# Weights converted ahead of the first scores, and places of their own for the beginning and for each batch's preparation

## The chip, the core and the metric

The kernel runs on one core of a Trainium2 chip. A core has five engines with instruction queues of their own: TensorE (PE: matmuls; its weight loads are shown as PEld), VectorE (DVE), ScalarE (ACT), GpSimd (POOL) and SyncE (SP), which here only issues DMA transfers. SBUF is the working memory with 128 partitions; matmuls write to PSUM, of which a partition has eight banks of 2 KB. Each engine takes its instructions in the order in which they were recorded and waits on semaphores for what it needs. The metric is the time of one execution on the device in microseconds (us), the median of three runs.

## The reference

Two layers follow each other, for 4 batches of 12288 positions with 128 channels. The first is an attention over 768 pooled positions that serve as keys and values at once, the second a gated feed-forward layer with a token shift.

```python
kv_pool = kv.reshape(B, H // r, r, W // r, r, C).mean(axis=(2, 4))     # r = 4: means over 16
k = v = kv_pool.reshape(B, -1, C) @ w_sr                               # 768 x 128 a batch
s = (q @ k.transpose(0, 2, 1)) / sqrt(C)
a = exp(s - s.max(-1, keepdims=True)); a /= a.sum(-1, keepdims=True) + 1e-9
x = a @ v
x_prev = x shifted by one position (0 in front)
xk = mu_k * x + (1 - mu_k) * x_prev;  xr = mu_r * x + (1 - mu_r) * x_prev
k = maximum(xk @ w_k, 0);  v = (k * k) @ w_v                           # 128 -> 1024 -> 128
out = v / (1 + exp(-(xr @ w_r)))
```

The feed-forward weights come in double precision; all else is single precision.

## The kernel before, in words

Precision is kept by splitting: a factor is held as a high part in the format fp32r, which TensorE takes at full rate, and a low part that is the remainder (names end in h and l). A product is then three matmuls, low x high, high x low, high x high. The probabilities are split into two fp16 halves (pp), the values into v1 and v2.

A batch is cut into 24 tiles of 512 positions, 96 tiles in all. For one tile (plan_tile):

- qf is loaded and split into qh (ScalarE) and ql (GpSimd). For each of four groups of 128 positions, S0 to S3 (six matmuls: three over 512 keys, three over 256) give the scores in PSUM. VectorE takes the negated maximum nm, ScalarE the exponential pe with its sum, VectorE the reciprocal (dn, rc), ScalarE the first half of the probabilities (f1) and VectorE the second (f2: scalar_tensor_tensor into pp). A DMA transposes pp into pT (tt).
- AV0 to AV5 (18 matmuls px<-pT,v) form the attention's output. ScalarE scales it into xe, VectorE forms the differences d, xk and xr and the high part xkh, ScalarE xrh, GpSimd the low parts xkl and xrl.
- ha and hb (24 matmuls ph<-...) form the hidden layer in four pairs of 128 rows. ScalarE takes the Relu rr and its square kh in fp32r, VectorE the product of ph and rr (the square, kk), and kk - kh = kl comes from GpSimd (from VectorE in the fourth pair).
- z (three matmuls pz<-...) forms the gate, worked out by ScalarE and VectorE (g). va and vb (24 matmuls pv<-...) form the second product; VectorE multiplies it by g into o, which a DMA stores.

A tile is 93 matmuls. PSUM is used in three pools: ps_b has three buffers of two banks for all big results (S, ph, pk, pt), ps_x one bank (px and pz), ps_v one bank (pv). A new tile of ps_b takes the buffer of an earlier one and waits until its last reader is done.

The order is written out by hand: the table WHEN gives each step a time, step s of tile i is recorded at i x PERIOD + WHEN[s] (note, plan: a heap sorted by time), and every engine executes in the order of recording. At any time TensorE works on four tiles: scores of one, px of the one before, ph and pv of older ones. The numbers only order the steps; nothing waits for a time.

Beside the tiles stand three more things, written as generators that yield waiting times (steps, until):

- batch_prep(0), the beginning: first_keys loads the first batch's windows in 16 loads; VectorE adds the two windows of each (two), TensorE multiplies by w_sr into pk, split makes ks, ksh and ksl.
- weights / load_weights: a part of 512 columns of w_k, w_v (two parts each) or 128 of w_r comes as pairs of 32-bit words. VectorE forms exponent and mantissa (e, ef, ei, m, six instructions), ScalarE the low word as a number (lf) and the high part (hi), GpSimd three instructions: rest, dw = top - hi, lo = dw + rest. w_k is converted from WK_AT on, w_v and w_r after the first S.
- batch_prep(1) to (3): later_keys loads the next batch's windows in 12 parts, one in each of 12 tiles, and VectorE adds them (acc<-kv_t); then pk (TensorE), ks (ScalarE), ksh (VectorE), ksl (GpSimd), the scale (am, ex, exi, exs, ivs, sv: one column but for am), ksv, the transposes pt (TensorE), and v1 (ScalarE) and v2 (VectorE) out of them. pk and pt are both put at the phase PK_AT of a tile.

All recorded steps have one line, that of the helper Ordered (L33), so the rows below are told apart by names.

Of the kernel before, what the change touches and what calls it, by code (L numbers as in the profile page):

```python
# [20 lines left out]
class Ordered:  # L21


    on = True

# [3 lines left out]
    def __getattr__(self, name):  # L29
        op = getattr(self.engine, name)  # L30

        def call(*args, **kwargs):
            ins = op(*args, **kwargs)  # L33
            return self.tc.keep_in_program_order(ins) if Ordered.on else ins

        return call
# [3 lines left out]
def tile_kernel(ctx, tc, qT, kv0, kvw, w_sr, mu_k, mu_r, w_k, w_v, w_r, outT):  # L40
    nc = tc.nc
    P = 128
# [38 lines left out]
    def load_weights(raw, hi, lo, half, gap):  # L81

        n = raw.shape[1]
        l32, h32 = raw[:, :, 0], raw[:, :, 1]
        e = work.tile([P, n], I32, name="e", tag="rr", bufs=2)
        dve.tensor_scalar(e, h32, 20, 0x7FF, op0=ALU.logical_shift_right, op1=ALU.bitwise_and)
        lf = work.tile([P, n], F32, name="lf", tag="kl", bufs=3)
        act.activation(out=lf, in_=l32.bitcast(mybir.dt.uint32), func=AF.Copy, scale=2.0 ** -52)
        yield gap
        least = 897.0 if half else 896.0  # L90
        ef = work.tile([P, n], F32, name="ef", tag="kh", bufs=3)
        dve.tensor_scalar(ef, e, least, least + 255.0, op0=ALU.max, op1=ALU.min)
# [12 lines left out]
        yield gap
        top = m.bitcast(F32)
# [9 lines left out]
    def split(c0, c1, pk, ks, ksh, ksl):  # L116

        act.activation(out=ks[:, c0:c1], in_=pk[:, c0:c1], func=AF.Copy, scale=scale / WIN)
        dve.tensor_copy(out=ksh[:, c0:c1], in_=ks[:, c0:c1])
        dve.tensor_tensor(  # L120
            out=ksl[:, c0:c1], in0=ks[:, c0:c1], in1=ksh[:, c0:c1].bitcast(F32), op=ALU.subtract
        )

    def first_keys(ks, ksh, ksl):

        pk = ps_b.tile([P, 1024], F32, name="pk", tag="big")
        for c0, c1 in CHUNKS:
            for w in range(0, WIN, 2):
                kv_t = prep.tile([P, 2, c1 - c0], F32, name="kv_t", tag="kv", bufs=KV_BUFS)
                sp.dma_start(out=kv_t, in_=kv0[:, w:w + 2, c0:c1])  # L130
                two = work.tile([P, T], F32, name="two", tag="az", bufs=2)[:, 0:c1 - c0]
                dve.tensor_tensor(out=two, in0=kv_t[:, 0, :], in1=kv_t[:, 1, :], op=ALU.add)
                pe.matmul(pk[:, c0:c1], lhsT=wsr, rhs=two, start=(w == 0), stop=(w == WIN - 2))
                yield 1.0
            split(c0, c1, pk, ks, ksh, ksl)

    def later_keys(b, ks, ksh, ksl):

        acc = prep.tile([P, K], F32, name="acc", tag="acc")
        for c0 in range(0, K, KC):  # L140
            kv_t = prep.tile([P, KC, WIN], F32, name="kv_t", tag="kv", bufs=KV_BUFS)
            sp.dma_start(out=kv_t, in_=kvw[b - 1, :, c0:c0 + KC, :])
            yield until(BR_AT, 6.0)
            dve.tensor_reduce(out=acc[:, c0:c0 + KC], in_=kv_t, axis=AX.X, op=ALU.add)
        yield until(PK_AT, 4.0)
        pk = ps_b.tile([P, 1024], F32, name="pk", tag="big")
        for c0, c1 in CHUNKS:
            pe.matmul(pk[:, c0:c1], lhsT=wsr, rhs=acc[:, c0:c1], start=True, stop=True)
        yield 2.0
        act.activation(out=ks, in_=pk[:, 0:K], func=AF.Copy, scale=scale / WIN)  # L150
        yield 3.0
        dve.tensor_copy(out=ksh, in_=ks)
        yield 3.0
        pool.tensor_tensor(out=ksl, in0=ks, in1=ksh.bitcast(F32), op=ALU.subtract)

    def batch_prep(b, res):

        later = b > 0
        ks = prep.tile([P, K], F32, name="ks")
        ksh = bat.tile([P, K], F32R, name="ksh")  # L160
        ksl = bat.tile([P, K], F32R, name="ksl")
        yield from later_keys(b, ks, ksh, ksl) if later else first_keys(ks, ksh, ksl)
        res += [ksh, ksl]
        yield V_WAIT if later else 4.0
        am = prep.tile([P, 1], F32, name="am")
        dve.tensor_reduce(out=am, in_=ks, axis=AX.X, op=ALU.max, apply_absolute_value=True)
        yield 3.0
        ex = prep.tile([P, 1], F32, name="ex")
        dve.tensor_scalar_max(ex, am, 2.0 ** -90)
        yield 2.0  # L170
        exi = prep.tile([P, 1], I32, name="exi")
        dve.tensor_single_scalar(exi, ex.bitcast(I32), 0x7F800000, op=ALU.bitwise_and)
        yield 2.0
        exs = prep.tile([P, 1], F32, name="exs")
        dve.tensor_scalar_mul(exs, exi.bitcast(F32), 2.0 ** -14)
        yield 2.0
        ivs = prep.tile([P, 1], F32, name="ivs")
        dve.reciprocal(ivs, exs)
        sv = bat.tile([P, 1], F32, name="sv")
        dve.tensor_scalar(sv, exs, 2.0 ** -15, 1.0 / scale, op0=ALU.mult, op1=ALU.mult)  # L180
        yield 2.0
        ksv = prep.tile([P, K], F32, name="ksv", tag="acc")
        dve.tensor_scalar_mul(ksv, ks, ivs)
        yield until(PK_AT, 4.0) if later else 2.0
        v1 = bat.tile([P, NK, P], F16, name="v1")
        v2 = bat.tile([P, NK, P], F16, name="v2")
        pt = ps_b.tile([P, 8, P], F32, name="pt", tag="big")
        for j in range(NK):
            pe.transpose(pt[:, j, :], ksv[:, j * P:(j + 1) * P], ident)
        yield 1.3 if later else 0.0  # L190
        act.copy(out=v1, in_=pt[:, :NK, :])
        yield 1.0 if later else 0.0
        dve.tensor_tensor(out=v2, in0=pt[:, :NK, :], in1=v1, op=ALU.subtract)
        res += [v1, v2, sv]

    plan = []
    now = [0.0]
# [6 lines left out]
    def steps(when, gen):  # L204

        def step():
            wait = next(gen, None)
            if wait is not None:
                steps(now[0] + wait, gen)
        note(when, step)  # L210

    def until(phase, least):

        return least + (phase - now[0] - least) % PERIOD

    def plan_tile(i, b, t):

        st = {}

        def at(when, least=-math.inf):  # L220
            def take(fn):
                note(max(i * PERIOD + when, least), fn)
            return take
# [5 lines left out]

        @at(WHEN["qf"], WHEN["S0"] if i else -math.inf)  # L230
        def _():
            sp.dma_start(out=new("qf", [P, T], F32), in_=qT[b, :, t * T:(t + 1) * T])

        @at(WHEN["qh"], WHEN["S0"] + 0.1 if i else -math.inf)
        def _():
            act.copy(out=new("qh", [P, T], F32R), in_=st["qf"])

        @at(WHEN["ql"])
        def _():
            pool.tensor_tensor(  # L240
                out=new("ql", [P, T], F32R), in0=st["qf"], in1=st["qh"].bitcast(F32), op=ALU.subtract
            )

        for s in range(NSUB):
            @at(WHEN[f"S{s}"])
# [12 lines left out]
            @at(WHEN[f"nm{s}"])  # L258
# [6 lines left out]
            @at(WHEN[f"ex{s}"])  # L265
# [6 lines left out]
            @at(WHEN[f"dn{s}"])  # L272
# [15 lines left out]
            @at(WHEN[f"f2{s}"])  # L288
# [6 lines left out]
            @at(WHEN[f"tt{s}"])  # L295
# [8 lines left out]
        for j in range(NK):  # L304
            @at(WHEN[f"AV{j}"])
# [164 lines left out]
    def weights(gap, *what):  # L470
# [8 lines left out]
        for part in parts:  # L479
            yield from load_weights(*part)  # L480
# [113 lines left out]
```

## Time and profile before

| | |
|---|---|
| median of three runs | 2014.72 us (2014.58 to 2014.96) |
| profiled execution, its own time | 2014.93 us |
| its span, first to last instruction | 2013.2 us |
| TensorE busy | 1966.7 us (98%), 8996 matmuls |
| VectorE busy | 1800.9 us (89%) |
| ScalarE busy | 1810.1 us (90%) |
| GpSimd busy | 1080.7 us (54%) |
| TensorE's share of the chain of waits | 93% |

The profile is one execution taken by the hardware profiler. Busy time is the union of an engine's instruction spans. A row of the timeline gives the start in us, the length in us, the engine, the operation, its output and inputs by the program's names, the count, and in brackets the engine's idle time before it with what ended it. Matmuls are pipelined, so the length of a matmul holds its way through the array; the distance of two starts is what it takes of the engine. TensorE's granted clock is given per window as a share of full speed (2.4 GHz; its other level is 1.2 GHz).

### The profile page before, as it was taken

Reading aid. Unit: us, or ns where it says so; the run is one execution under the profiler, and the core shown is the slowest. Engines: PE = TensorE matmul, PEld = TensorE weight load, DVE = VectorE, ACT = ScalarE, POOL = GpSimd, SP = SyncE. Lnnn points to the kernel's source line nnn. Section 1 sums busy time; section 2 is a strip of 40 time slices with the busy share of each in tenths; the row PEclk is TensorE's granted clock in tenths of the full one; section 3 lists DMA queues with packets and bytes.
Section 4 is the critical chain, followed back from the end, with each engine's and each line's share of the span. In section 5 each row is a group of like instructions: output and inputs, shape, how many; then the busy total and the mean of one; then the engine's idle time right before and its main releaser. Section 6 shows DMA issues by size and latency. Waiting matters only on the chain.

```text
span 2013.2 us, 27575 instructions
## 1 busy us (share of the span) xinstructions
PE 1966.7 (98%) x8996; PEld 1430.8 (71%) x8996; DVE 1800.9 (89%) x2809; ACT 1810.1 (90%) x2612; POOL 1080.7 (54%) x600
## 2 busy tenths in 40 slices
PE   5899999999999999999999999999999999999999
PEld 2577777777777777677777777777777777777776
DVE  6899999889899999988989999988989898989896
ACT  2799999899999999889999999989999999999997
POOL 3455555555464646545555555555555554646455
PEclk7899999999999999999999999999999999999999
DMA  6565755455566666554647575645555555555542
GB/s 207 115 138 117 151 118 114 86 110 100 110 131 131 131 131 121 106 102 91 121 91 152 119 140 124 130 84 110 100 110 100 110 100 110 100 110 100 110 89 58
DMA packets 640591, 230.61 MB, mean 115 GB/s; under 512 B 606400, under 2 KB 608704, under 8 KB 640448
## 3 DMA queue, kind: packets, MB, share of 16 engines
q1 hardware_dynamic: 640448, 228.85, 55.6%
q8 instruction: 72, 1.18, 0.2%
q14 instruction: 71, 0.58, 0.1%
HBM read 52.63 MB, written 25.17 MB: 39 GB/s over the span
## 4 chain that ended last, share of the span: by engine, by line
PE 93%; ACT 2%; DVE 1%; issue 0%; DVEq 0%; ACTq 0%
PE ph L33 26%; PE pv L33 26%; PE S L33 20%; PE px L33 19%; PE pz L33 3%; ACT kh L33 1%; ACT rr L33 0%; DVE kk L33 0%; ACT xe L33 0%; DVE pp L33 0%; DVE v L33 0%; DVE ph L33 0%; DVE kl L33 0%; ACT ks L33 0%; ACT v L33 0%
## 5 line engine op out<-in xcount | busy, mean ns | idle before, releaser
L33 POOL TENSOR_TENSOR kl<-kk,kh 128x1024 fp32r<-128x1024 f32 x288 | 694.3, 2411 | 794.4 <-ACT kh L33 786.7
L33 PE MATMUL px<-pT,v 128*128 128x512 f16 x1728 | 474.4, 384 | 4.4 <-DMA pT<-pp 4.4
L33 ACT ACTIVATE rr<-ph 128x1024 f32<-128x1024 f32 x384 | 382.5, 1022 | 102.3 <-PE ph L33 101.8
L33 DVE TENSOR_TENSOR kk<-ph,rr 128x1024 f32<-128x1024 f32 x288 | 350.5, 1218 | 76.8 <-ACT rr L33 75.1
L33 ACT ACTIVATE kh<-rr 128x1024 fp32r<-128x1024 f32 x384 | 406.0, 1058 | 11.9
L33 DVE SCALAR_TENSOR_TENSOR pp<-pe,rc,pp 128x768 f16<-128x768 f32 x384 | 381.9, 1015 | 26.7 <-ACT pp L33 26.1
L33 DVE TENSOR_REDUCE nm<-S 128x1 f32<-128x768 f32 x384 | 364.9, 950 | 17.9 <-PE S L33 17.9
L33 ACT ACTIVATE pe<-S,nm 128x768 f32<-128x768 f32 x384 | 346.8, 903 | 18.8 <-DVE nm L33 11.1
L33 PE MATMUL ph<-xkh,wkl 128*128 128x512 f32 x768 | 357.0, 465 | 5.1 <-ACT pe L33 4.1
L33 ACT ACTIVATE pp<-pe,rc 128x768 f16<-128x768 f32 x384 | 347.3, 933 | 11.8 <-ACT pe L33 11.2
L33 PE MATMUL pv<-kh,wvl 128*128 128x512 f32 x768 | 306.0, 398 | 0.2 <-DVE o L33 0.2
L33 PE MATMUL ph<-xkh,wkh 128*128 128x512 f32 x768 | 304.4, 396 | 0.0
L33 PE MATMUL pv<-kh,wvh 128*128 128x512 f32 x768 | 303.8, 396 | 0.0
L33 PE MATMUL S<-ksh,ql 128*128 128x512 f32 (+1 forms) x768 | 281.5, 367 | 14.4 <-DVE v L33 7.3
L33 PEld LDWEIGHTS <-v 128*128 128x128 f16 x1728 | 123.7, 98 | 207.3 <-issue 135.7
L33 PE MATMUL S<-ksh,qh 128*128 128x512 f32 (+1 forms) x768 | 261.1, 340 | 0.0
L33 PE MATMUL S<-ksl,qh 128*128 128x512 f32 (+1 forms) x768 | 260.9, 340 | 0.1
L33 PE MATMUL ph<-xkl,wkh 128*128 128x512 f32 x768 | 244.4, 419 | 0.0
L33 PE MATMUL pv<-kl,wvh 128*128 128x512 f32 x768 | 243.3, 419 | 0.0
L33 PEld LDWEIGHTS S<-ksh,ql 128*128 128x128 f32 x768 | 145.6, 190 | 59.7 <-DVE v L33 8.6
L33 PEld LDWEIGHTS ph<-xkh,wkl 128*128 128x128 f32 x768 | 145.1, 189 | 58.3 <-ACT pe L33 4.3
L33 PEld LDWEIGHTS pv<-kl,wvh 128*128 128x128 f32 x768 | 145.2, 189 | 41.1 <-POOL kl L33 0.5
(79 smaller groups left out, 2822.2 us busy)
## 6 DMA issues: line engine op xcount, KB each, us to landing
qf<-qT SPq DMA_DIRECT2D x96, 256.0 KB, 3.5
outT<-o SPq DMA_DIRECT2D x96, 256.0 KB, 3.2
kv_t<-kvw SPq DMA_DIRECT2D x36, 512.0 KB, 4.4
pT<-pp SPq DMA_TRANSPOSE x384, 4.0
kv_t<-kv SPq DMA_DIRECT2D x8, 512.0 KB, 7.4
kv_t<-kv SPq DMA_DIRECT2D x8, 256.0 KB, 3.9
raw<-moe_w_k SPq DMA_DIRECT2D x2, 512.0 KB, 6.4
raw<-moe_w_v SPq DMA_DIRECT2D x2, 512.0 KB, 6.6
```

Of the source, the lines that this page charges most:

```text
L33: ins = op(*args, **kwargs)
```

## The change

1. load_weights is written as single steps, each with a place in a table ONCE. The parts of w_k and the first of w_v now have places ahead of the first S, w_r and the second part of w_v among the first tiles. The masked value top is written to PSUM (a bank of ps_x or ps_v in turn), and VectorE forms top - hi there and adds rest; GpSimd keeps only rest.
2. The beginning (first_keys): the pair sums are gone for the first 512 keys, whose 16 windows TensorE multiplies one by one; for the other 256 keys a load has four windows, which VectorE adds in one instruction (four). The two ranges have a pk of their own. All steps and loads have places in ONCE.
3. The first five tiles take their places from a table EARLY, one for each; WHEN (rounded to two digits) holds from the sixth tile on.
4. The steps of a later batch's preparation have places in a table PREP; the key sums stay where they were.

```diff
-    def load_weights(raw, hi, lo, half, gap):
...
-        act.copy(out=hi, in_=top)
-        rest = work.tile([P, n], F32, name="rest", tag="kh", bufs=3)
-        pool.tensor_tensor(out=rest, in0=lf, in1=ei.bitcast(F32), op=ALU.mult)
-        d = work.tile([P, n], F32, name="dw", tag="kl", bufs=3)
-        pool.tensor_tensor(out=d, in0=top, in1=hi.bitcast(F32), op=ALU.subtract)
-        pool.tensor_tensor(out=lo, in0=d, in1=rest, op=ALU.add)
+    def once(name):
+        def take(fn):
+            note(ONCE[name], fn)
+        return take
+    def load_weights(c, name, w, hi, lo, half, top_pool, top_tag):
...
+        @once(f"wt{c}")
+        def _():
+            st["top"] = top_pool.tile([P, T], F32, name="top", tag=top_tag)[:, :n]
+            dve.tensor_tensor(
+                out=st["top"].bitcast(I32), in0=st["m"], in1=st["ei"], op=ALU.bitwise_or
+            )
+        @once(f"wq{c}")
+        def _():
+            st["rest"] = scratch("rest", "kh", [P, n], F32)
+            pool.tensor_tensor(
+                out=st["rest"], in0=st["lf"], in1=st["ei"].bitcast(F32), op=ALU.mult
+            )
+        @once(f"wh{c}")
+        def _():
+            act.copy(out=hi, in_=st["top"])
+        @once(f"wd{c}")
+        def _():
+            dve.tensor_tensor(
+                out=st["top"], in0=st["top"], in1=hi.bitcast(F32), op=ALU.subtract
+            )
+        @once(f"wo{c}")
+        def _():
+            dve.tensor_tensor(out=lo, in0=st["top"], in1=st["rest"], op=ALU.add)
...
     def first_keys(ks, ksh, ksl):
-        pk = ps_b.tile([P, 1024], F32, name="pk", tag="big")
-        for c0, c1 in CHUNKS:
-            for w in range(0, WIN, 2):
-                kv_t = prep.tile([P, 2, c1 - c0], F32, name="kv_t", tag="kv", bufs=KV_BUFS)
-                sp.dma_start(out=kv_t, in_=kv0[:, w:w + 2, c0:c1])
-                two = work.tile([P, T], F32, name="two", tag="az", bufs=2)[:, 0:c1 - c0]
-                dve.tensor_tensor(out=two, in0=kv_t[:, 0, :], in1=kv_t[:, 1, :], op=ALU.add)
-                pe.matmul(pk[:, c0:c1], lhsT=wsr, rhs=two, start=(w == 0), stop=(w == WIN - 2))
+        for i in range(WIN // 2):
+            @once(f"L_a{i}")
...
+                for j in range(2):
+                    pe.matmul(
+                        st["pk"][:, 0:512], lhsT=wsr, rhs=st[f"a{i}"][:, j, :],
+                        start=(st["a"] == 0), stop=(st["a"] == WIN - 1),
+                    )
...
+        for i in range(WIN // 4):
...
+                dve.tensor_reduce(
+                    out=st[f"s{i}"], in_=st[f"b{i}"].rearrange("p w k -> p k w"), axis=AX.X,
+                    op=ALU.add,
+                )
...
+        def at(name):
+            def take(fn):
+                note((i0 + PREP_AT) * PERIOD + PREP[name] if later else ONCE[name], fn)
+            return take
...
-        yield until(PK_AT, 4.0) if later else 2.0
...
     def plan_tile(i, b, t):
         st = {}
-        def at(when, least=-math.inf):
+        places = EARLY[i] if i < len(EARLY) else WHEN
+        def at(name):
             def take(fn):
-                note(max(i * PERIOD + when, least), fn)
+                note(places[name] + (0.0 if i < len(EARLY) else i * PERIOD), fn)
             return take
...
-PK_AT = 64.0
...
+PREP = {
+    "pk": -2.945, "ks": -0.264, "am": 1.413, "ksh": 13.567, "ex": 22.909, "exi": 25.299,
...
+ONCE = {
+    "L_wk0": 57.612, "L_a0": 57.862, "we0": 58.362, "L_a1": 58.612, "L_a2": 58.862,
...
+EARLY = [
+    {
+        "qf": 65.862, "qh": 66.862, "ql": 68.612, "S0": 82.112, "nm0": 83.862, "S1": 84.112,
...
```

The order of each engine from the sixth tile on is the old one but for the preparations. TensorE at the second batch's pk (acc are the summed windows, pv<-kh the second product), before:

```order
L33 MATMUL ph<-xkl,wkh 128x512 x2
L33 MATMUL pk<-acc,wsr 128x512
L33 MATMUL pk<-acc,wsr 128x256
L33 MATMUL pv<-kh_3299,wvl 128x512
L33 MATMUL pv<-kh_3299,wvh 128x512
L33 MATMUL pv<-kh_3299,wvl 128x512
L33 MATMUL pv<-kh_3299,wvh 128x512
L33 MATMUL S<-ksh,ql 128x512
```

The same product now:

```order
L31 LDWEIGHTS v_95
L31 MATMUL px<-pT,v_95 128x512
L31 MATMUL pk<-acc,wsr 128x512
L31 MATMUL pk<-acc,wsr 128x256
L31 MATMUL S<-ksh,ql 128x512
L31 MATMUL S<-ksl,qh 128x512
```

It stood between the hidden layer and the second product, four matmuls ahead of a tile's first S; it now stands between a px and the tile's last S. TensorE at the second batch's transposes (pt, six of 128 columns), before:

```order
L33 MATMUL ph<-xkl,wkh 128x512 x2
L33 MATMUL pt<-ident,ksv 128x128 x6
L33 MATMUL pv<-kh_3759,wvl 128x512
L33 MATMUL pv<-kh_3759,wvh 128x512
L33 MATMUL pv<-kh_3759,wvl 128x512
L33 MATMUL pv<-kh_3759,wvh 128x512
L33 MATMUL S<-ksh,ql 128x512
```

The transposes now:

```order
L31 MATMUL pv<-kl_3855,wvh 128x512 x2
L31 MATMUL pv<-kl_3866,wvh 128x512 x2
L31 MATMUL pt<-ident,ksv 128x128 x6
L31 LDWEIGHTS v_95
L31 MATMUL px<-pT,v_95 128x512
L31 LDWEIGHTS v_96
L31 MATMUL px<-pT,v_96 128x512
L31 LDWEIGHTS v_95
L31 MATMUL px<-pT,v_95 128x512
L31 MATMUL ph<-xkh,wkl 128x512
```

They stood four matmuls ahead of a first S too; the next user of a big PSUM buffer behind them is now a ph, three px later. VectorE before the first S (top and the differences with wkh and wvh are weights, four the sums of four windows), now:

```order
L31 TENSOR_TENSOR top<-m,ei 128x512
L31 TENSOR_TENSOR top<-top,wkh 128x512
L31 TENSOR_REDUCE four<-kv_t 128x256
L31 TENSOR_TENSOR wkl<-top,rest 128x512
L31 TENSOR_TENSOR top<-m,ei 128x512
L31 TENSOR_TENSOR top<-top,wkh 128x512
L31 TENSOR_TENSOR top<-top,wvh 128x512
L31 TENSOR_REDUCE four<-kv_t 128x256
L31 TENSOR_TENSOR wvl<-top,rest 128x512
L31 TENSOR_REDUCE four<-kv_t 128x256 x2
L31 TENSOR_TENSOR wkl<-top,rest 128x512
L31 CAST ksh<-ks 128x512
```

Before, the same engine had there:

```order
L33 TENSOR_TENSOR two<-kv_t 128x512 x8
L33 CAST ksh<-ks 128x512
L33 TENSOR_TENSOR ksl<-ks,ksh 128x512
L33 TENSOR_TENSOR two<-kv_t 128x256 x5
L33 TENSOR_SCALAR e<-raw 128x512
L33 TENSOR_SCALAR ef<-e 128x512
L33 TENSOR_TENSOR two<-kv_t 128x256
L33 TENSOR_SCALAR ei<-ef 128x512
```

The first weight part came behind 13 of the 16 pair sums; now three weight parts are done ahead of the first keys (ksh). SP's first loads change with it: a part of w_k is the first load, and q loads and weight parts stand between the key loads, which wait for free buffers (KV_BUFS = 6).

## Rows read from the trace of the kernel before

**Rows 1.** Timeline of TensorE: start, length; the first gate matmul of five tiles.

```profile
310.09 0.39 PE L33 MATMUL pz<-xrh,wrl 128*128 128x512 f32 x1
...
332.52 0.39 PE L33 MATMUL pz<-xrh,wrl 128*128 128x512 f32 x1
...
352.57 0.39 PE L33 MATMUL pz<-xrh,wrl 128*128 128x512 f32 x1
...
377.26 0.63 PE L33 MATMUL pz<-xrh,wrl 128*128 128x512 f32 x1
...
397.60 0.39 PE L33 MATMUL pz<-xrh,wrl 128*128 128x512 f32 x1
```

**Rows 2.** Timeline at the second batch's pk and pt; brackets: idle time before, releaser.

```profile
326.30 1.45 PE L33 MATMUL pk<-acc,wsr 128*128 128x512 f32 x4
...
329.50 0.50 PE L33 MATMUL S<-ksh,ql 128*128 128x512 f32 x1 [0.81 <-ACT ks L33]
...
368.78 0.82 PE L33 MATMUL pt<-ident,ksv 128*128 128x128 f32 x6
...
371.95 0.96 DVE L33 TENSOR_TENSOR v<-pt,v 128x768 f16<-128x768 f32 x1 [1.55 <-ACT v L33]
...
372.96 0.50 PE L33 MATMUL S<-ksh,ql 128*128 128x512 f32 x1 [2.43 <-DVE v L33]
...
375.99 0.63 PE L33 MATMUL pv<-kh,wvh 128*128 128x512 f32 x1
```

**Rows 3.** Windows: length, busy us (instructions) per engine, PEclk, DMA share, GB/s.

```profile
0.00:20.00 20.00, 10.92 (x16) 3.51 (x16) 7.26 (x11) 3.06 (x4) 1.96 (x7) 0.99 0.92 326
20.00:40.00 20.00, 13.35 (x37) 8.85 (x38) 17.89 (x33) 5.23 (x11) 10.14 (x7) 0.67 0.45 143
40.00:60.00 20.00, 8.12 (x30) 6.29 (x30) 18.63 (x33) 10.02 (x17) 9.71 (x7) 0.59 0.47 92
```

**Rows 4.** Timeline, marks of the beginning.

```profile
5.52 0.96 DVE L33 TENSOR_TENSOR two<-kv_t 128x512 f32<-128x512 f32 x1 [5.52 <-DMA kv_t<-kv]
...
28.81 0.58 PE L33 MATMUL S<-ksh,ql 128*128 128x512 f32 x1
...
52.59 1.95 DVE L33 SCALAR_TENSOR_TENSOR pp<-pe,rc,pp 128x768 f16<-128x768 f32 x2
...
59.30 4.00 PE L33 MATMUL px<-pT,v 128*128 128x512 f16 x9 [4.35 <-DMA pT<-pp]
...
73.83 0.62 PE L33 MATMUL ph<-xkh,wkl 128*128 128x512 f32 x1 [4.09 <-ACT pe L33]
```

**Rows 5.** Timeline of an undisturbed tile, where pk and pt stand now.

```profile
319.81 0.59 PE L33 MATMUL S<-ksh,ql 128*128 128x512 f32 x1
320.20 1.22 DVE L33 TENSOR_TENSOR kk<-ph,rr 128x1024 f32<-128x1024 f32 x1 [0.46 <-ACT rr L33]
...
321.34 0.95 DVE L33 TENSOR_REDUCE nm<-S 128x1 f32<-128x768 f32 x1
...
322.35 0.91 ACT L33 ACTIVATE pe<-S,nm 128x768 f32<-128x768 f32 x1
...
323.12 0.58 PE L33 MATMUL ph<-xkh,wkl 128*128 128x512 f32 x1
```

**Rows 6.** Timeline: weight conversion beside GpSimd, alone, and a key sum.

```profile
28.09 1.45 POOL L33 TENSOR_TENSOR dw<-m,wkh 128x512 f32<-128x512 f32 x1
28.33 1.49 DVE L33 TENSOR_SCALAR e<-raw 128x512 int32<-128x512 int32 x1
...
32.14 0.42 DVE L33 TENSOR_SCALAR m<-raw 128x512 int32<-128x512 int32 x1
...
33.20 0.69 DVE L33 TENSOR_TENSOR m<-m,ei 128x512 int32<-128x512 int32 x1
...
296.30 1.21 DVE L33 TENSOR_REDUCE acc<-kv_t 128x64 f32<-128x1024 f32 x1
```

**Rows 7.** The page's first row: busy us, share of the span, instructions.

```profile
PE 1966.7 (98%) x8996; PEld 1430.8 (71%) x8996; DVE 1800.9 (89%) x2809; ACT 1810.1 (90%) x2612; POOL 1080.7 (54%) x600
```

More of the change, by code (lines that the diff above doesn't have):

```diff
@@ L137, in later_keys @@
[L137 to L183, printed above, removed]
-        yield until(PK_AT, 4.0) if later else 2.0
[L185 to L194, printed above, removed]
@@ L202, in note, with scratch @@
         heapq.heappush(plan, (when, next(count), fn))
[L204 to L214, printed above, removed]
+    def once(name):
+        def take(fn):
+            note(ONCE[name], fn)
+        return take
+    def scratch(name, tag, shape, dtype):
+        return work.tile(shape, dtype, name=name, tag=tag, bufs=BUFS.get(tag, 2))
@@ new lines, in later_keys, with part, load, add @@
+    def later_keys(b, i0, at, ks, ksh, ksl):
+        st = {}
+        def part(n):
+            c0 = n * KC
+            def load():
+                if n == 0:
+                    st["acc"] = prep.tile([P, K], F32, name="acc", tag="acc")
+                st[n] = prep.tile([P, KC, WIN], F32, name="kv_t", tag="kv", bufs=KV_BUFS)
+                sp.dma_start(out=st[n], in_=kvw[b - 1, :, c0:c0 + KC, :])
+            def add():
+                dve.tensor_reduce(
+                    out=st["acc"][:, c0:c0 + KC], in_=st[n], axis=AX.X, op=ALU.add
+                )
+            when = (i0 + SUM_AT + n) * PERIOD + WHEN["br"] % PERIOD
+            note(when - 8.0, load)
+            note(when, add)
+        for n in range(K // KC):
+            part(n)
+        @at("pk")
+        def _():
+            st["pk"] = ps_b.tile([P, 1024], F32, name="pk", tag="big")
+            for c0, c1 in CHUNKS:
+                pe.matmul(st["pk"][:, c0:c1], lhsT=wsr, rhs=st["acc"][:, c0:c1], start=True, stop=True)
+        @at("ks")
+        def _():
+            act.activation(out=ks, in_=st["pk"][:, 0:K], func=AF.Copy, scale=scale / WIN)
+        @at("ksh")
+        def _():
+            dve.tensor_copy(out=ksh, in_=ks)
+        @at("ksl")
+        def _():
+            pool.tensor_tensor(out=ksl, in0=ks, in1=ksh.bitcast(F32), op=ALU.subtract)
@@ L216, in plan_tile @@
     def plan_tile(i, b, t):
         st = {}
-        def at(when, least=-math.inf):
+        places = EARLY[i] if i < len(EARLY) else WHEN
+        last = max((f"v{x}{f}" for x in "ab" for f in range(NF // 2)), key=places.get)
+        def at(name):
             def take(fn):
-                note(max(i * PERIOD + when, least), fn)
+                note(places[name] + (0.0 if i < len(EARLY) else i * PERIOD), fn)
             return take
@@ L444, in _ @@
                         st["pv"], lhsT=wvh[:, fs], rhs=kh,
-                        start=False, stop=(V_LAST == f"va{f}" and i == 1),
+                        start=False, stop=(last == f"va{f}" and i == 1),
                     )
-            @at(WHEN[f"vb{f}"])
+            @at(f"vb{f}")
             def _(f=f):
@@ L512 @@
 XRH_ON = 'act'
-BR_AT = 15.59
-PERIOD = 20.2
+SUM_AT = 5
+PREP_AT = 18
 BUFS = {
```

306 lines of the change are left out of this document (206 added, 100 removed), and 138 rows, old and new, of tables (EARLY, ONCE, WHEN).

## The prediction

> **What bounds the kernel now.** I read first the starts of one matmul that every tile has once, the first gate matmul (pz<-xrh,wrl) [rows 1]: they lie 20.05 us apart (352.57 to 332.52), and TensorE has no idle time between. So the end moves only by what happens before the tiles run at this distance, or where the distance is broken. Both are in the trace.
>
> The distance is broken at each of the three later batches' preparations, twice: 310.09 to 332.52 is 22.43, and 352.57 to 397.60 is 45.03 for two tiles, 4.93 over 40.10. The timeline of these places [rows 2] gives the reason. The keys' product pk stands ahead of an S, whose PSUM buffer comes free only when ScalarE has copied pk (0.81 us idle). The transposes pt stand before another S, which waits 2.43 us for VectorE's second half of the values; after that idle time matmuls of 512 columns take 0.63 us, not 0.39, so TensorE runs at the lower of its two clock levels for a while. One batch costs 2.38 + 4.93 = 7.31 us over the plain distance, three cost 21.9.
>
> The beginning I read by 20 us windows [rows 3]. TensorE is busy 10.9, 13.4 and 8.1 of 20 us, at a granted clock of 0.67 and 0.59 in the second and third. VectorE is busy 7.3, 17.9 and 18.6: idle while the first keys come, then full. So from 20 us on the beginning is bound by VectorE: weights, keys and softmax in one queue. The marks [rows 4]: first key load in use at 5.52, first S at 28.81, last remainder of tile 0 done at 54.54 (52.59 + 1.95), its first px at 59.30 (the transposing DMA lands 4.76 later), the first ph, by which the fill ends, at 73.83.
>
> **The change part by part: a later batch's preparation.** Its instructions stay the same (12 key sums, pk, ks, ksh, ksl, the scale, ksv, pt, v1, v2); only places move. pk goes ahead of the tile's last S, pt behind the values' products that follow it. I set them into the undisturbed tile [rows 5]. With three big PSUM buffers, pk takes the one that this S had, and S must wait until VectorE has squared the first ph (320.20 + 1.22 = 321.42). pk itself is 1.45 with the drain of its last matmul, about 1.2 of TensorE's order. S could go at 319.81 + 1.2 = 321.01 and goes at 321.42: 0.4 of waiting, 1.6 in all.
>
> For pt: ksv and its reciprocal stand on VectorE before that square, some 0.95 + 0.15 (nearest row: another pass over 768 columns, 0.95), of which 0.46 falls into an idle gap. The chain square, maximum, exponential is 0.64 later; the exponential ends at 323.26 + 0.64 = 323.90, and the next ph, which takes the buffer of that S, would go at 323.12 + 0.6 (pt without drain) = 323.72. So 0.2 to 0.3 of waiting, 0.9 in all. v1 and v2 then have until the next tile's S, over 3 us later, so the 2.43 goes and with it the clock's fall.
>
> What is late next is VectorE: the maximum of the keys (am, 0.95) and v2 (0.96) push the squares by about 1 us each in one tile. Queued behind them are the o product and the second halves of the probabilities, for which TensorE waits a quarter of a tile later. I take 0.3 for it. Sum 1.6 + 0.9 + 0.3 = 2.8 against 7.31: 4.5 per batch, 13.6 for three. Bounds: TensorE's own work only (1.8) gives 16.5; the old waits met again at the new places give 0; more than that is excluded, since the instructions and their releases are the same ones.
>
> **The beginning.** Added on VectorE: per 512 columns of weight, a subtraction and an addition of 0.69 (nearest row the 0.69 of m<-m,ei [rows 6]), three parts ahead of the first S. Removed there: 16 pair sums; four sums over four windows take their place (1.21, the key sums' row, as many elements). The other key products go to TensorE unsummed, 16 matmuls for 8. That costs TensorE nothing in the end, since it waits in this stretch anyway; without that cover, at the lower level, some 10 us more.
>
> GpSimd loses two instructions per part. While its dw ran (28.09 to 29.54) VectorE's e took 1.49 us and ended with it, against 0.42 for a like m alone [rows 6], so they held each other up; I charge 1 us for what GpSimd still has there. The Trainium skill says in Advanced Engine Details and Errata (the note on the second Vector SBUF port) that two-port VectorE instructions and GpSimd's block each other on that port; the trace agrees in these rows. By that rule the new subtraction and addition, each with one operand in PSUM, would not be held, and the sum would be 1 us lower; by the row, were each held like e, it would be some 6 higher.
>
> When the first S goes: the third weight part has 3.74 MB asked for up to it, the first key load had 0.85 and was in use at 5.52; at 326 GB/s [rows 3] the part is there at 5.52 + 8.9 = 14.4. From there VectorE has no reason to wait: three parts at 4 x 0.42 + 4 x 0.69 = 4.4, less 3.5 done by then, and four sums of 1.21, are 14.7. With the 1 for GpSimd this gives 30. (The last loads wait for buffers: the last b load stands in SP's queue behind a q load, which waits for GpSimd's remainder of tile 1; by the same rows it lands at about 26.5 and just holds.) So S goes about 1 us later than now, but with three of four big weight parts done; now one is done by then and three follow among the softmax.
>
> From there by VectorE's order to the last remainder of tile 0: 6 maxima (0.95) 5.7, 4 remainders (0.97) 3.9, am, ksv and v2 2.9, splitting the keys 1.8, the small part of wr 1.5, some 15 instructions on one column (0.15) 2.3: 18.1, so 48.1, and px at 52.9. Then 6 maxima, 4 remainders, the rest of the weights 3.6, d, xk, xr, xkh 2.7, 14 small ones 2.1: 18.0 to xkh. One wait of 0.5 for xe: first ph at 66.6, against 73.83. By then TensorE has two S groups (2 x 1.06) and three px (0.7) more behind it than now, 2.8 of work. 7.2 + 2.8 = 10.0. From there on TensorE has 158 matmuls to tile 1's gate (now 157), VectorE its usual load. The five tiles' own order has px of tile 1 ahead of tile 0's ph and one PSUM bank for both; I take 1.4 for such waits. Gain of the beginning: 8.6. Bounds: 12.6 (loads 2.5 earlier, nothing lost after) and, with the pk stretch at the lower level (10) and 3 of waits, a loss of 3.
>
> **The sum.** 2014.93 (span 2013.2 and 1.7 around it) - 13.6 - 8.6 = 1992.7; the profiled run lies 0.2 above the median of the runs shown, so 1992.5. The end is untouched: the last tiles' order is the old one.
>
> **Rivals.**
> A, the fill gives nothing: VectorE does no less work in all, and its idle 12 us at the start may come back as waits on loads. Against it: rows 3 and the order show two parts drawn into that idle time. Only the preparations count: 2001.3.
>
> B, the preparations' waits only move: the square and the exponential that then free the buffers are late, TensorE idles over 2 us again and falls to the lower level. For it: VectorE is busy 89% of the span [rows 7], so what it does late stays late for a while. Against it: the places' slack above. Only the beginning counts: 2006.1.
>
> C, every cover holds: 12.6 and 16.5, 1985.6.
>
> D, the slower side: the clock. Between the first S and tile 1's gate TensorE waits for VectorE again and again and stays at the lower level, as it did at 0.59 in the third window. The 158 matmuls behind the first ph are 34 us of work at a tile's rate (93 in 20.05); at half the clock they take 34 more: 2026.5. It decides once it costs over 22 of these 34. Against it: now the first ph starts at the lower level too, and the tiles reach 20.05 at once.
>
> E, the places make no difference, since TensorE's total is the bound: 2014.7. Rows 2 speak against it, its waits are in that total.
>
> **How the numbers follow.** Chances: the forecast 0.52 (own range 1986 to 1999), A 0.15, B 0.12, C 0.12, D 0.06, E 0.03. The range 1982 to 2006.5 holds the first four but half of B. A measurement of this kernel tells about 0.2%, 4 us, from no change: faster by more 0.91, within 0.03, slower 0.06.
>
> **What would show it.** Right: gate starts 21.7 and 21.0 apart where they are 22.43 and 24.69, no idle time over 1 us on TensorE there, granted clock 1.00; first S near 30, first px of tile 0 near 53, first ph near 67, gate distance 20.05 from tile 5 on. Wrong: a wait of over 2 us for a square or an exponential at pk or pt (B); VectorE idle over 3 us between 14 and 30, or granted clock under 0.7 past the first ph (A, D).

## The result and the profile after

The changed kernel takes 1993.39 us (median of 5 runs, 1992.74 to 1994.28) against 2014.72 of the kernel before (5 runs, 2014.58 to 2015.27): the ratio is 0.9894, 95% interval 0.9879 to 0.9908. It is faster by 21.3 us; the forecast was 1992.5. The profiled execution has a span of 1991.2 us against 2013.2, 22.0 less.

First the starts of the gate matmul [rows 1], now (timeline of TensorE: start, length):

```profile
323.73 0.39 PE L31 MATMUL pz<-xrh,wrl 128*128 128x512 f32 x1
...
345.33 0.39 PE L31 MATMUL pz<-xrh,wrl 128*128 128x512 f32 x1
...
365.39 0.39 PE L31 MATMUL pz<-xrh,wrl 128*128 128x512 f32 x1
...
386.07 0.39 PE L31 MATMUL pz<-xrh,wrl 128*128 128x512 f32 x1
```

The two long distances are 21.60 and 20.68, where 22.43 and 24.69 stood. Over 20.05 that is 1.55 + 0.63 = 2.18 a batch for 7.31: 5.13 gained, and 15.4 in three (the other two batches read 21.62 and 20.69, 21.60 and 20.68). The places themselves [rows 2], now:

```profile
333.63 1.45 PE L31 MATMUL pk<-acc,wsr 128*128 128x512 f32 x4
335.12 0.19 PEld L31 LDWEIGHTS S<-ksh,ql 128*128 128x128 f32 x1 [0.43 <-DVE kk L31]
335.12 0.50 PE L31 MATMUL S<-ksh,ql 128*128 128x512 f32 x1
...
377.95 0.82 PE L31 MATMUL pt<-ident,ksv 128*128 128x128 f32 x6
378.60 0.81 PE L31 MATMUL px<-pT,v 128*128 128x512 f16 x3
...
379.63 0.96 DVE L31 TENSOR_TENSOR v<-pt,v 128x768 f16<-128x768 f32 x1
...
382.23 0.39 PE L31 MATMUL pv<-kh,wvl 128*128 128x512 f32 x1
383.16 0.39 PE L31 MATMUL S<-ksh,ql 128*128 128x512 f32 x1
```

No idle time stands in brackets on TensorE's matmuls any more; at pk only the weights of the next S wait 0.43 for VectorE's square (kk). VectorE's second half of the values (v) is done at 380.59, the next S comes 2.6 us later, and 512 columns take 0.39 after pt, where they took 0.63: the clock stays up (granted 1.00 from 360 to 380 us, 0.91 in the kernel before).

The rest lies in the beginning. Its windows [rows 3] and the next four (length, busy us and instructions of PE, PEld, DVE, ACT, POOL, granted clock, DMA share, GB/s):

```profile
0.00:20.00 20.00, 10.21 (x19) 4.26 (x20) 10.24 (x19) 4.26 (x6) 2.00 (x7) 1.00 0.85 281
20.00:40.00 20.00, 15.68 (x53) 8.73 (x51) 18.62 (x33) 5.94 (x13) 4.99 (x4) 0.91 0.58 201
40.00:60.00 20.00, 15.77 (x73) 11.61 (x72) 19.37 (x40) 16.52 (x30) 4.26 (x3) 0.91 0.85 159
60.00:80.00 20.00, 13.72 (x53) 8.64 (x54) 17.70 (x32) 14.14 (x20) 10.88 (x6) 0.83 0.75 144
80.00:100.00 20.00, 19.33 (x88) 13.71 (x87) 19.25 (x24) 17.98 (x26) 10.54 (x7) 1.00 0.39 86
100.00:120.00 20.00, 19.89 (x93) 14.47 (x92) 17.66 (x29) 17.04 (x25) 11.77 (x6) 1.00 0.67 134
120.00:140.00 20.00, 18.58 (x87) 13.52 (x87) 18.12 (x30) 17.26 (x26) 8.68 (x6) 1.00 0.55 121
```

VectorE is fuller in the first three (10.2, 18.6, 19.4 for 7.3, 17.9, 18.6), and the clock is 0.91 where it was 0.67 and 0.59. What is new is TensorE's idle time from 80 to 140: 2.20 us, before none. The marks [rows 4], now:

```profile
5.82 0.43 DVE L31 TENSOR_SCALAR e<-raw 128x512 int32<-128x512 int32 x1 [5.82 <-DMA raw<-moe_w_k]
...
33.25 0.47 PE L31 MATMUL S<-ksh,ql 128*128 128x512 f32 x1 [0.31 <-DVE ksh L31]
...
46.91 1.02 DVE L31 SCALAR_TENSOR_TENSOR pp<-pe,rc,pp 128x768 f16<-128x768 f32 x1
...
53.55 2.76 PE L31 MATMUL px<-pT,v 128*128 128x512 f16 x12
...
65.80 1.44 PE L31 MATMUL px<-pT,v 128*128 128x512 f16 x3 [6.08 <-DVE pp L31]
66.67 0.99 PE L31 MATMUL ph<-xkh,wkl 128*128 128x512 f32 x1
...
81.46 0.40 PE L31 MATMUL pz<-xrh,wrl 128*128 128x512 f32 x1
...
183.35 0.39 PE L31 MATMUL pz<-xrh,wrl 128*128 128x512 f32 x1
```

First S 4.4 us later than before, last remainder of tile 0 at 47.93 (54.54), first ph 7.16 earlier, gate of tile 0 at 81.46 (89.50). At tile 5, the first with the general places, the gate is at 183.35 (189.77): 6.42 gained. 15.4 + 6.4 = 21.8 of the 22.0. TensorE's sum [rows 7] now:

```profile
PE 1959.5 (98%) x9004; PEld 1425.6 (72%) x9004; DVE 1801.8 (90%) x2807; ACT 1808.3 (91%) x2612; POOL 1074.7 (54%) x590
```

### The profile page after: what moved, and what is told of

The parts are those of the page before. It is cut to its first block, busy times and chain, and to the rows that moved or that the text cites. A ratio compares the mean times of both kernels' runs of the same rounds, so it can differ in the third digit from the quotient of the medians.

```text
span 1991.2 us, 27581 instructions
## 1 busy us (share of the span) xinstructions
PE 1959.5 (98%) x9004; PEld 1425.6 (72%) x9004; DVE 1801.8 (90%) x2807; ACT 1808.3 (91%) x2612; POOL 1074.7 (54%) x590
## 4 chain that ended last, share of the span: by engine, by line
PE 94%; DVE 4%; ACT 1%; DMA 1%; issue 1%; SPq 0%; DVEq 0%; ACTq 0%
PE ph L31 26%; PE pv L31 26%; PE S L31 19%; PE px L31 19%; PE pz L31 3%; DMA kv_t<-kv 1%; DVE nm L31 1%; PE pk L31 1%; DVE kk L31 1%; DVE pp L31 0%; ACT rr L31 0%; DVE kl L31 0%; DVE ph L31 0%; DVE xkh L31 0%; ACT pp L31 0%
## 5 line engine op out<-in xcount | busy, mean ns | idle before, releaser
L31 ACT ACTIVATE pe<-S,nm 128x768 f32<-128x768 f32 x384 | 346.6, 903 | 23.0 <-DVE nm L31 13.6
L31 ACT ACTIVATE pp<-pe,rc 128x768 f16<-128x768 f32 x384 | 348.3, 933 | 15.5 <-ACT pe L31 10.2
L31 POOL TENSOR_TENSOR xkl<-xk,xkh 128x512 fp32r<-128x512 f32 x96 | 124.9, 1301 | 93.4 <-DVE xkh L31 91.8
```

The source lines that it names most:

```text
L31: return self.tc.keep_in_program_order(op(*args, **kwargs))
```

## The experiments

The kernels ran on several chips; each ratio is against runs of the kernel before on the same chip, with its 95% interval. My theory: two independent gains, a wait that is gone at pt, and a beginning in which VectorE is kept full.

**The two halves.** The new beginning with the old places of the preparations, and the old beginning with the new ones; from the sixth tile on each engine's order is exactly that of the one or the other kernel.

```diff
 PREP = {
-    "pk": -2.945, "ks": -0.264, "am": 1.413, "ksh": 13.567, ... "pt": 39.938, "v1": 41.544, ...
+    "pk": -16.8, "ks": -14.8, "ksh": -11.8, "ksl": -8.8, "am": 7.2, ... "pt": 23.6, "v1": 24.9, ...
```

> The new beginning with every step of the later batches' preparations back at its old place (the order of each engine from there on is that of the kernel before). Theory: the preparations' gain is local, 7.31 us over the plain distance before and 2.18 after (gate starts 21.60 and 20.68 apart), 5.13 each, 15.4 for three: 1993.4 + 15.4 = 2008.8. Rival 1, the new beginning is what lets the tiles run without waits at the preparations: below 2000. Rival 2, the beginning gives nothing without the places: 2014.

> The old beginning with the new places of the later preparations alone (order of each engine behind the beginning as in the changed kernel). Theory: 2014.7 - 15.4 = 1999.3, and the two halves add up: this kernel and the one with the old places together lie as far from the kernel before as the changed one, within 1 us. Rival: halves that overlap, so that this one alone reaches 1995 or less, or one that needs the other, 2005 or more.

Measured: 2007.68 (ratio 0.9963, 0.9950 to 0.9975) and 2000.86 (0.9929, 0.9917 to 0.9942). Of 2014.7 that is 7.4 for the beginning and 14.3 for the preparations, 21.7 together, and both together gave 21.4. They add up within the intervals, which reach about 2.5 us to either side. With the old places (prep_old) the old distances are back, 22.42, 20.05 and 24.95 between these rows:

```profile
304.69 0.39 PE L31 MATMUL pz<-xrh,wrl 128*128 128x512 f32 x1
...
327.11 0.39 PE L31 MATMUL pz<-xrh,wrl 128*128 128x512 f32 x1
...
347.16 0.39 PE L31 MATMUL pz<-xrh,wrl 128*128 128x512 f32 x1
...
372.11 0.40 PE L31 MATMUL pz<-xrh,wrl 128*128 128x512 f32 x1
```

In this run's last preparation the same wait passed without the lower clock, in one execution:

```profile
1336.00:1356.00 20.00, 17.57 (x84) 12.92 (x83) 16.41 (x28) 16.50 (x26) 10.95 (x6) 1.00 0.37 80
...
1344.53 0.50 PE L31 MATMUL S<-ksh,ql 128*128 128x512 f32 x1 [2.44 <-DVE v L31]
```

The distance there is 23.40, where it is 24.95 with a granted clock of 0.91. So of the 4.9 us that pt's old place costs, about 1.5 are the clock.

**pk and pt apart.**

```diff
# pk_old
-    "pk": -2.945, "ks": -0.264,
+    "pk": -16.8, "ks": -14.8,
# pt_old
-    "ex": 22.909, ... "ksv": 39.066, "pt": 39.938, "v1": 41.544, "v2": 42.543,
+    "ex": 14.0, ... "ksv": 18.2, "pt": 23.6, "v1": 24.9, "v2": 25.9,
```

> The changed kernel with only the keys' product pk and its copy ks at their old place (a tile's first S four matmuls behind it); all else of the preparation at the new places. Theory: pk costs 2.38 there and 1.55 at the new place, 0.83 a batch: 1993.4 + 2.5 = 1995.9, gate starts 22.4 apart where 21.60 stand and 20.68 as now at pt. Rival 1, pk's place works through VectorE's queue on pt too (pt alone at its old place cost 16.6, both together 14.3): pk alone at its old place would then cost nothing or less, 1993.4 or below. Rival 2, it brings the lower clock: 1998 or more.

> The changed kernel with only the scale, the transposes pt and the values v1 and v2 at their old place; pk stays at the new one. Theory: pt's place makes 4.93 of the 7.31, of which 0.63 is left now: 4.30 per batch, 12.9 for three, 2006.3; a wait of about 2.4 us of an S for v2 and matmuls of 0.63 us behind it come back. Rival 1, the wait at pt came from pk's old place, by VectorE's queue: below 1996. Rival 2, the wait comes back without the lower clock: 2.43 + 0.6 over the distance, 1993.4 + 3 x 2.4 = 2000.6.

pk alone: 1995.94 (0.9913, 0.9899 to 0.9927), gate starts 303.68, 326.10: 22.42, and 20.69 at pt, as the theory had it. pt alone: 2010.05 (0.9974, 0.9964 to 0.9985), 3.7 more than the theory, and by the median more than both at their old places (2007.68; the intervals of the two ratios overlap). Its rows:

```profile
361.98 0.82 PE L31 MATMUL pt<-ident,ksv 128*128 128x128 f32 x6
...
366.09 0.96 DVE L31 TENSOR_TENSOR v<-pt,v 128x768 f16<-128x768 f32 x1 [1.34 <-ACT v L31]
...
367.10 0.57 PE L31 MATMUL S<-ksh,ql 128*128 128x512 f32 x1 [3.39 <-DVE v L31]
...
371.66 0.39 PE L31 MATMUL pz<-xrh,wrl 128*128 128x512 f32 x1
```

The wait is 3.39 where the kernel before has 2.43, and the distance to the gate before it (345.76) is 25.90, where it is 24.95 with both at their old places. Counted from tile 5's gate (183.79 here, 184.37 in prep_old), pt comes at 178.19 and 179.01, TensorE being 0.82 earlier here, but v2 at 182.30 and 182.17 and the S behind it at 183.31 and 183.18. So v2 hangs on ScalarE and VectorE, not on TensorE, and what TensorE had saved at pk it waits for at pt. pk's new place is worth 2.5 us only because pt no longer waits. The rest of the difference between the two profiles comes from the last preparation: there the granted clock is 0.83 (from 1336 to 1356 us) and the distance 26.85, against 1.00 and 23.40 in prep_old. Why v2 is 0.13 later is not settled; this kernel also has the scale's small steps and ksh nearer to pt.

**The first tiles' own places, and the weights ahead of the first S.** Once the general table for all tiles, and once the first part of w_v converted behind the first S.

```diff
# early_when (EARLY = [], and all of ONCE 37.9 earlier, so that the first S keeps its place among them)
-                note(places[name] + (0.0 if i < len(EARLY) else i * PERIOD), fn)
+                least = {"qf": 44.21, "qh": 44.31}.get(name, 0.0) if i else 0.0
+                note(max(places[name] + i * PERIOD, least), fn)
# wv0_late (and its top in the other PSUM bank)
-    "L_wv0": 61.612, "we2": 64.362, "wf2": 66.112, ... "wd2": 76.862, "wo2": 77.612,
+    "L_wv0": 75.500, "we2": 96.000, "wf2": 96.200, ... "wd2": 98.200, "wo2": 98.600,
```

> The changed kernel whose first five tiles take the general table (spaced 20.2) in place of their own; the keys, the weights and their places ahead of the first S stay. Theory: first S near 33 as now; from it to tile 0's gate the kernel before took 60.7 us with about 6 us more of weight conversion on VectorE in it, so 54 to 55 here, gate of tile 0 near 88 (81.46 in the changed kernel, 89.50 before), and 4 of the beginning's 6.4 us are the tiles' own places: 1997.5. Rival 1, the places give nothing and the weights all of it: 1993.4. Rival 2, the places give all and the weights nothing: 1999.8 or more.

> The changed kernel with the first part of w_v converted behind the first S (between the parts of w_r and the second of w_v, whose work on VectorE is 0.42 x 4 + 0.69 x 4 = 4.4 with the waits for it; its load goes behind the last key load). Theory: VectorE waits 3.8 us for weight loads and 1 for key loads ahead of the first S, and this part fills part of that; 0.5 MB less ahead of the keys brings the first S 2 earlier (31.3), but the 4.4 come back among the softmax of the first tiles, where VectorE is full: first ph 1 to 2.4 later than 66.67, time 1994.4 to 1995.8. Rival 1, it makes no difference where the part stands (VectorE's total sets the first ph): 1993.4. Rival 2, the loads ahead of the keys are what costs: first S 2 earlier and the time with it, 1991.4.

early_when: 1997.70 (0.9913, 0.9899 to 0.9927), by the median what was expected: 4.3 more than the changed kernel. By the medians, then, the own places are worth 4.3 and the weights ahead of the first S about 2.0 (2015.06 - 1997.70 - 15.4). Its profile, of the longest of the five runs, has the gate of tile 0 at 88.84 and of tile 5 at 189.11, against 89.50 and 189.77 in the kernel before: 0.7 for the weights and 5.8 for the own places in that execution. But its first S goes at 35.46, 2.2 later than in the changed kernel. The general table also issues the q load of tile 0 first, at 1.19, ahead of the first weights, so the edit changes the loads as well. From the first S to the gate of tile 5 it takes 3.6 more than the changed kernel. Its first S and its windows:

```profile
35.46 0.47 PE L31 MATMUL S<-ksh,ql 128*128 128x512 f32 x1 [0.32 <-DVE ksh L31]
...
40.00:60.00 20.00, 11.15 (x43) 8.88 (x44) 15.74 (x35) 11.72 (x21) 3.95 (x3) 0.67 0.46 92
60.00:80.00 20.00, 16.00 (x65) 9.80 (x64) 15.17 (x31) 12.70 (x23) 3.78 (x3) 0.85 0.67 114
```

VectorE idles 4.3 and 4.8 us in the two windows, for S and for ScalarE. The closer tiles of the own table put maxima and remainders into that time (19.37 and 17.70 above). wv0_late: 1994.80 (0.9904, 0.9889 to 0.9920), inside the expected range, though its interval overlaps the changed kernel's: first S 3.2 earlier (30.02), first ph 0.8 later (67.45), gate of tile 0 at 83.08. So this part, ahead of the first S, delays it by 3.2 us and pays 4.9 back by tile 0's gate (81.46 with it). The net of 1.6 at the gate is not far above the 1.0 by which executions of one order differ from the first S to that gate (last section).

**What sets the first S.** Sums of another form, another order on TensorE, and remainders on GpSimd again. A fourth kernel has tile 0's first ph ahead of tile 1's px.

```diff
# four_kc (with the input laid out so, and one product pk at the end)
-                st[f"b{i}"] = prep.tile([P, 4, K - 512], F32, name="kv_t", ...
+                st[f"b{i}"] = prep.tile([P, KC, WIN], F32, name="kv_t", ...
-                    out=st[f"s{i}"], in_=st[f"b{i}"].rearrange("p w k -> p k w"), axis=AX.X,
+                    out=st["four"][:, i * KC:(i + 1) * KC], in_=st[f"b{i}"], axis=AX.X,
# pa7_first
-    "pa7": 78.362,
+    "pa7": 77.000,
# pool_rem (top in SBUF)
-            dve.tensor_tensor(out=st["top"], in0=st["top"], in1=hi.bitcast(F32), ...
+            pool.tensor_tensor(out=st["top"], in0=st["top"], in1=hi.bitcast(F32), ...
-            dve.tensor_tensor(out=lo, in0=st["top"], in1=st["rest"], op=ALU.add)
+            pool.tensor_tensor(out=lo, in0=st["top"], in1=st["rest"], op=ALU.add)
# ph_first, tile 1
-        "AV0": 111.830, "AV1": 112.255,
+        "AV0": 112.500, "AV1": 112.550,
```

> The changed kernel with the last 256 keys of the first batch laid out like the later batches' (64 keys with their 16 windows next to each other), so that VectorE's four sums are of the form 128x64 from 128x1024, and one product pk of 256 columns at the end in place of four. Theory: the four sums took 1.9 each because they walk across windows 1 KB apart, the later batches' take 1.21; VectorE is the bound, so first S 4 x 0.7 = 2.8 earlier (30.5 for 33.25) and about as much of it at the end: 1990.6. Rival 1, the loads bind: VectorE waits longer for the next load, first S near 32.5, 1992.8. Rival 2, the sums' time is of the element count, 1.9 again: 1993.4.

> The changed kernel with TensorE's last two key products of the first 512 keys moved ahead of the product of the second sum, behind which they stand from 25 to 28.4 us. Theory: the first keys' half (ks) is ready some 4 us earlier, but VectorE is full until the last sum, so first S at 32.7 to 33.3 and the time 1993.4 within 0.6. Rival: TensorE's waiting (2.73 us, then matmuls at the lower clock until 31.6) sets the first S: 30.3, and 1990.5.

> The changed kernel with the weights' remainders formed in SBUF by GpSimd again (subtraction and addition, two more of its instructions per part) at the same places; VectorE loses six instructions of 0.69 ahead of the first S (4.1 us) and four behind it. Theory: a VectorE instruction with two inputs in SBUF is held while GpSimd's runs (top took 1.65 and 1.79 for 0.69 beside rest), so each of GpSimd's six new 1.27 us costs VectorE up to 1.1; three of the six meet such an instruction: 4.1 - 3.3, first S at 32.5 and the time 1993 within 1.5. Rival 1, no such meeting: first S 4.1 earlier, 1989.5. Rival 2, all are held: 1996 or more.

> The changed kernel with tile 0's first four ph matmuls ahead of tile 1's first px, which waits 6.08 us until 65.80 for its transposed probabilities. Theory (the 1.4 that the forecast took for such waits): xkh is done at 64.74, so first ph at 64.8 for 66.67, and 1 to 1.9 of it stays to the end: 1992. Rival: the wait is taken by the next thing that VectorE is late with (second halves of the probabilities, kk): 1993.4.

four_kc: 1991.74 (0.9889, 0.9875 to 0.9904). The sums take 1.22 for 1.94, but first S comes 0.84 earlier in the profiled executions, not 2.8. By these rows rival 1 (the loads) holds, for the last key load goes at 24.87 and VectorE waits 2.11 for it; the time lies midway between the theory's 1990.6 and that rival's 1992.8:

```profile
21.19 3.58 SPq L31 DMA_DIRECT2D qf<-qT  x2
...
24.87 0.38 SPq L31 DMA_DIRECT2D kv_t<-kvb  x1
...
30.11 1.22 DVE L31 TENSOR_REDUCE four<-kv_t 128x64 f32<-128x1024 f32 x1 [2.11 <-DMA kv_t<-kvb]
...
32.41 0.77 PE L31 MATMUL S<-ksh,ql 128*128 128x512 f32 x1
```

pa7_first: 1994.06 (0.9901, 0.9887 to 0.9916), first S at 33.65: nothing, as expected. pool_rem: 1992.73 (0.9891, 0.9875 to 0.9908), first S at 33.67. The time is the expected one, but not for the reason given: the second to fourth sums ran beside GpSimd at 1.9 to 2.0 each, no longer than alone, and a cast was held (1.05 for 0.42); what VectorE saves it waits for a load:

```profile
25.71 1.27 POOL L31 TENSOR_TENSOR rest<-lf,ei 128x512 f32<-128x512 f32 x1
26.29 3.87 DVE L31 TENSOR_REDUCE four<-kv_t 128x256 f32<-128x1024 f32 x2 [5.37 <-DMA kv_t<-kv]
...
32.48 1.05 DVE L31 CAST ksh<-ks 128x512 fp32r<-128x512 f32 x1
```

So the remainders in PSUM give no time that these runs can show. ph_first: 1994.13 (0.9902, 0.9887 to 0.9917). Its first ph goes 0.57 after the start of xkh (66.11 to 65.54), in the changed kernel 2.35 after it (66.67 to 64.32); first S was at 34.45, so from first S to the gate of tile 0 it takes 47.67 for 48.21. Half a microsecond at most, not the expected 1 to 1.9: the matmuls that follow wait for VectorE (0.48 for wvl at 79.16, 0.38 at 88.15, 0.28 at 90.10, as in the changed kernel).

**Two further steps.** The q loads of tiles 2 and 3 behind the last key load, and ksh from ScalarE.

```diff
# four_kc_q: four_kc and, for tiles 2 and 3
-        "qf": 73.112,
+        "qf": 76.200,
-        "qf": 73.612,
+        "qf": 76.250,
# four_kc_q_act: also (at 78.700 and 80.620 in ONCE, behind ks)
-                dve.tensor_copy(out=ksh[:, c0:c1], in_=ks[:, c0:c1])
+                act.activation(out=ksh[:, c0:c1], in_=st["pk2" if n else "pk"][:, 0:c1 - c0],
+                    func=AF.Copy, scale=scale / WIN)
```

> The kernel with the sums of 64 keys, and the q loads of tiles 2 and 3 behind the last key load in SyncE's queue (they stood ahead of it; the first of them waited for GpSimd, and the last key load went at 24.87 and held VectorE for 2.11 us). Theory: the load queue sets the first S; the last key load goes at about 21.3, VectorE has no wait there, first S at 30.4 (32.41 without this step, 33.25 in the changed kernel) and 2 us of it stay: 1989.7. Rival 1, the loads share a rate that is used up (350 to 400 GB/s there), so another load is late in its place: 1991.7 as without the step. Rival 2, VectorE waits for TensorE or GpSimd next, first S at 31.5: 1990.8.

> As four_kc_q, and the high part of the first batch's keys (ksh) comes from PSUM by ScalarE, which is idle there, in place of VectorE's casts (0.42 + 0.29). Theory: VectorE is full from the last sum to the first S, so first S 0.7 earlier again (29.7) and 1989.0. Rival: ScalarE's two passes over 512 and 256 columns (0.60 and 0.38) stand in the chain pk, ks, ksh, ksl, and take the place of the casts: 1989.7 as without it.

four_kc_q: 1991.64 (0.9885, 0.9867 to 0.9903), first S at 30.29, 0.1 from the theory; the gate of tile 0 gained only 0.7 on four_kc, though, and the time is that of rival 1, as without the step. four_kc_q_act: 1990.22 (0.9881, 0.9865 to 0.9896), the lowest median; first S no earlier (30.63: ScalarE's passes replace the casts in the chain, the rival). Its gate of tile 0 is 1.2 ahead of four_kc_q's; that VectorE's 0.7 us, free behind the first S, are part of it is argued, not shown:

```profile
30.63 0.99 PE L31 MATMUL S<-ksh,ql 128*128 128x512 f32 x1
...
78.58 0.40 PE L31 MATMUL pz<-xrh,wrl 128*128 128x512 f32 x1
```

Its gate of tile 0 is 2.88 ahead of the changed kernel's, its span 2.8 shorter (1988.4). The intervals of the two ratios overlap, so the times alone don't tell the two apart. The marks speak for it: in the four profiled kernels with the changed kernel's order up to that gate it lies between 81.46 and 82.50, here at 78.58.

## Why the prediction was right, step by step

- **pk: right.** 1.6 forecast, 1.55 measured, by the wait for VectorE's square that it named (0.43 on the weights of that S, for 0.4); pk_old confirms the price of the old place.
- **pt: right in kind, too dear.** 0.9 was forecast, 0.63 measured, just its own six transposes; the wait of 0.2 to 0.3 for the exponential did not come. Nor did the 0.3 of late work on VectorE. So 2.18 a batch, not 2.8, and 15.4 for three, not 13.6; the stated limit of 16.5 was nearer.
- **First S near 30: wrong, 33.25.** Two terms were too small. The four sums were priced by the key sums' 1.21 [rows 6], "as many elements"; they read each key's four windows 1 KB apart and took 1.9 to 2.0: 2.9 more. And VectorE, which had "no reason to wait" from 14.4 on, waited 1.2:

```profile
21.57 1.27 POOL L31 TENSOR_TENSOR rest<-lf,ei 128x512 f32<-128x512 f32 x1
21.61 1.79 DVE L31 TENSOR_TENSOR top<-m,ei 128x512 int32<-128x512 int32 x1
...
25.91 1.94 DVE L31 TENSOR_REDUCE four<-kv_t 128x256 f32<-128x1024 f32 x1 [1.03 <-DMA kv_t<-kv]
...
28.36 3.81 DVE L31 TENSOR_REDUCE four<-kv_t 128x256 f32<-128x1024 f32 x2
```

A cast of 0.42 (ksh) ahead of S was not in the sum either. These come to 4.5 for the 3.25 missed; most of the rest is that instructions in a full queue overlap (next point). The Trainium skill has the rule (Advanced Engine Details and Errata, SBUF Cachelines): accesses that each fall on another 16-byte line pay a penalty. The trace agrees: the same 1024 elements took 1.22 once they lay next to each other (four_kc). But four_kc changed the form too, from 256 sums of four to 64 sums of sixteen, so that the distance alone makes the difference is argued, not shown. The number of results seems to cost little: a maximum, one result from 768 elements, takes 0.95 [rows 5], 1.24 ns an element, and 64 sums from 1024 take 1.22, 1.19 ns.

- **Last remainder of tile 0 at 48.1: right (47.93), by luck: two errors cancel.** First S was 3.25 late, and VectorE needed 3.3 less from there. From 33.14 to 47.93 its 37 instructions have lengths that sum to 17.3, 0.8 less than the forecast's 18.1 (the first cast of ksh ran ahead of S, and ksv took 0.61); they took 14.79. A length holds 0.07 on average, 0.09 behind a pass of 512 or 768 columns, that lies beside the next instruction, so a sum of lengths is too long for a full queue.
- **px 52.9 and 2.8 us of work ahead: right** (53.55; two S groups and three px more stand ahead of the first ph). **First ph 66.6: right in the number (66.67), not in the path.** VectorE was done with xkh at 64.74, 1.9 before the forecast. The first ph then stood behind tile 1's px, which waited until 65.80 for its probabilities (6.08 idle). With ph ahead of that px it goes 0.57 after the start of xkh (ph_first).
- **1.4 lost to waits: too small.** TensorE idles 2.7 from the first ph to 140 us (0.48 before 80, then 0.67, 0.11, 1.42). 7.2 + 2.8 - 2.7 = 7.3, but 6.4 are measured. Most of the last 0.9 is in the waits too, by the starts: a bracket counts from the end of a matmul's length, which is 0.16 longer than its distance to the next start. At 87.48 a bracket of 0.39 stands for a distance of 0.78, where 0.23 is usual, and the next matmul follows after 0.35. So reckoned, an estimate, the four waits cost 3.4 where their brackets have 2.6. The beginning gained 6.4, not 8.6.
- **GpSimd's hold: about right.** 1 us was charged. After 14.4 one instruction was held: top, with both inputs in SBUF, took 1.79 beside rest (21.57 to 22.84) where it takes 0.69 alone. top - hi, with an input in PSUM, took 0.70 beside ql (23.74 to 25.01); that agrees with what the prediction drew from the Trainium skill (Advanced Engine Details and Errata, the note on the second Vector SBUF port). pool_rem, with the remainders back on GpSimd, has the same time, so this decides nothing here.
- **The sum**: 15.4 + 6.4 in place of 13.6 + 8.6. One part was 1.8 too small, the other 2.2 too large, so that the total came within 0.9 us is luck in part. Rivals B, C, D and E are refuted by the rows above (B: no wait over 0.5 at pk or pt; C: 2.2 of idle time from 80 to 140 us; D: clock 0.83 and more in each window of 20 us; E: both halves gain). A was right in part: the weights ahead of the first S, taken without the tiles' own places, gained 2.0 by the medians and 0.7 in the profiled execution.

## What to carry to other kernels

A stage can be moved to where the engines behind it have slack, and then costs its own work only; find the place by what is waited for next. A saving ahead of a fixed wait is given back at that wait (pt_old), so take the last wait of a stretch away first. In a beginning, work drawn ahead of the first result pays little (here some 2.0 of 6.4) until the later order fills the time that it leaves free on the bounding engine.

## What the runs showed that was not expected

- Sums over elements 1 KB apart: 1.94 us for 1024 elements a partition (256 sums of four), 1.22 with neighbours (64 sums of sixteen).
- VectorE instructions in a full queue start 0.07 us on average before the length of the one ahead has ended.
- The start differs between executions: five kernels have the same order up to the first S, and it came at 33.25 (changed kernel), 33.39 (pk_old), 33.53 (prep_old), 33.90 (pt_old) and 34.45 (ph_first). Tile 0's gate follows 47.6 to 49.0 us later in these and in four_kc, pa7_first and pool_rem. So a mark of the beginning that moved by less than about 1 us shows nothing by itself.
- Not all VectorE work beside GpSimd is held: sums (TENSOR_REDUCE, 1.93 beside it and 1.9 alone) and instructions with a PSUM input (0.70) were not; one with two inputs in SBUF (1.79 for 0.69) and a cast with one input in SBUF (1.05 for 0.42 in pool_rem) were.
- A wait of 2.44 us at pt's old place was followed by the lower clock in two of three preparations of prep_old, not in the third.
